# Two units' attention joined one unit earlier, with unit 19's transposing transfer ahead of two loads

## The chip, the cores and the metric

One core of a Trainium2 chip runs one launch of the kernel. The metric is the device time of that launch in microseconds; lower is better. A profiled execution gives, for each engine, when each instruction ran: TensorE (matrix products), VectorE, ScalarE, GpSimd, and SyncE, whose queue SP issues transfers.

## What is computed

Linear attention with a decay for each head, in blocks of 64 positions, followed by two matrix products with a leaky Relu between them. Batch 4, 8 heads, 768 positions, head size 64; then 3072 tokens, model width 512, hidden width 2048.

```python
for b in range(nb):
    sl = slice(b * block, (b + 1) * block)
    qb, kb, vb = (q[:, :, sl].copy(), k[:, :, sl].copy(), v[:, :, sl].copy())
    intra = np.einsum('bhic,bhjc->bhij', qb, kb) * Dmask[None]
    intra = np.einsum('bhij,bhjd->bhid', intra, vb)
    inter = np.einsum('bhid,bhde->bhie', qb * lam_pow[None], kv_state)
    out[:, :, sl] = intra + inter
    kb_dec = kb * rev_pow[None]
    kv_state = lam_block[None, :, None, None] * kv_state + np.einsum('bhsd,bhse->bhde', kb_dec, vb)
...
h = x @ w_in
g = np.maximum(h, 0.0) + alpha * np.minimum(h, 0.0)
return (g @ w_out).astype(np.float32)
```

## The kernel before

**Units and chunks.** The attention works on blocks of 128 positions, two of them (256 positions) at a time. A unit is one batch entry, one half of the heads (4 heads) and one such stretch of 256 positions; there are 24 units, numbered 0 to 23. Four units make a chunk `c` of 512 tokens: chunk 3 is units 12 to 15, chunk 4 is 16 to 19, chunk 5 is 20 to 23. The raw inputs are loaded for a pair of units, `load(c, bi, x)`; `(4, 0)` serves units 16 and 17, `(4, 1)` 18 and 19, `(5, 0)` 20 and 21, `(5, 1)` 22 and 23.

**The second part.** For chunk `c`, `up(c, f)` (L527) makes 128 of the 2048 hidden values for the chunk's 512 tokens: four matmuls into a PSUM bank, a Relu on ScalarE (L540), and on VectorE the operation that makes the leaky Relu `g` (L549). The bank is free when VectorE has read it. `down(c, t, part, 4)` (L556) makes a quarter of the output sums of 128 tokens: four matmuls with four of the sixteen `g`. Parts 0 to 3 of one `t` accumulate in the bank "op"; after part 3 ScalarE copies the sums to `o_sb` and SP stores them. Part `p` reads the `g` numbered 4p to 4p+3. A chunk's `up` needs the attention output `xT` of its four units; `down` of a chunk runs while the next chunk's `up` does.

**What a unit needs.** `prepared(n)` casts k, q and v to 16 bits (k and v on GpSimd, q on ScalarE) and makes the decayed keys on GpSimd. `turned(n)` transposes q and k with one DMA transfer on SP's queue into a tile `qkT` (three buffers, so unit n takes the one of unit n-3). `decayed(n)` multiplies the transposed q with the decay on GpSimd. `states` and `states2` carry the running states on VectorE.

**Stages of attention.** `cluster(old, new)` (L474) puts on TensorE the output of one unit and the scores and state products of another: inter-block products of `old` (L371), scores of `new` (L387), products of masked scores with v of `old` (L412), state products of `new` (L432). VectorE then masks the scores (L398), ScalarE copies the output to `xT`. `cluster2(olds, news)` (L676) does it for up to two old and two new units; the second new unit's scores go into the two "h" banks (L644) and are masked in two halves (L658). Before, `cluster(15, 16)` is the last stage with one new unit, and the joined stages are 16/17+18, 17+18/19+20, 19+20/21, 21/22+23 and 22+23/none.

**Banks.** PSUM has two banks "h" that rotate, one "op", one "tk", two for scores "s", and `acc` (two banks). The second accumulator of joined stages (`acc2`) takes "tk" from `second()` (L597) on.

**Order.** The program's order is written by hand and every engine runs its own instructions in that order; the tile framework inserts the waits. From chunk 3 on, a string of U and D gives the order of `up(c, ...)` and `down(c-1, ...)`, and a table gives what is issued ahead of a position ("step") in it: loads and `turned` on SP, casts on GpSimd and ScalarE, stages on TensorE. GpSimd, ScalarE, VectorE and SP each run in order, so a wait holds what is behind it on that engine.

Of the kernel before, what the change touches and what calls it, by code (L numbers as in the profile page):

```python
# [11 lines left out]
def kernel(  # L12
# [67 lines left out]
    def load(c, bi, x, half=None, queue="S"):  # L80

        pb, b = c // 2, 2 * (c % 2) + bi
        if (c, bi) not in raws:
            raws[c, bi] = [raw_pool.tile([128, H, 2 * D], fp32, tag=f"{n}raw", name=f"{n}raw") for n in "kqv"]
        heads = ds(0, H) if half is None else ds(4 * half, 4)
        i = "kqv".index(x)
        (nc.gpsimd if queue == "G" else nc.sync).dma_start(
            out=raws[c, bi][i][:, heads, :],
            in_=(k, q, v)[i][b, heads, ds(pb * W, W), :].rearrange("h (p e) d -> p h (e d)", e=2),
        )  # L90
# [191 lines left out]
    def engine(x):  # L282
        return nc.gpsimd if x == "G" else nc.vector
# [62 lines left out]
    def decayed(n, eng="G"):  # L346
        c, bi, hh = units[n]
        t = T[n]
        qdT = qkt_pool.tile([128, 2, 2, L], fp16, tag="qdT", name="qdT")
        p = ds(64, 64) if c < 2 else ds(0, L)  # L350
        engine(eng).tensor_tensor(  # L351
            out=qdT[:, :, :, p],
            in0=(t["qps"] if eng == "P" else t["qkT"][:, 0])[:, :, :, p],
            in1=qdecay[:, hh, :, :, p],
            op=ALU.mult,
        )
        t["qdT"] = qdT
# [6 lines left out]
    def inter(n):  # L364
        co, bo, ho = units[n]
        pbo, bb = co // 2, 2 * (co % 2) + bo
        for a in range(2):
            if 2 * pbo + a == 0:
                continue
            for hp in range(2):  # L370
                nc.tensor.matmul(  # L371
                    ot[a][:, hp, :].rearrange("p (e j) -> p e j", e=2),
                    lhsT=R[bb, ho, 2 * pbo + a][:, hp].rearrange("p l d -> p (l d)"),
                    rhs=T[n]["qdT"][:, :, hp, ds(a * 64, 64)],
                    start=(hp == 0),
                    stop=False,
                    skip_group_check=True,
                )

    def score_products(n):  # L380
        t = T[n]
        t["s"] = ps.tile([128, 2, 2, 2, L], fp32, tag="s", name="s")
        for hp in range(2):
            for e in range(2):
                for a, hl in QUADS:
                    p = ds(hl * 64, 64)
                    nc.tensor.matmul(  # L387
                        t["s"][ds(a * 64, 64), hl, hp, 1 - e, :].rearrange("p (e j) -> p e j", e=2),
                        lhsT=t["qkT"][p, 1, e, hp, ds(a * 64, 64)],
                        rhs=t["qkT"][p, 0, :, hp, ds(a * 64, 64)],  # L390
                        start=True,
                        stop=True,
                    )

    def masked(n):
        t = T[n]
        t["sm"] = sm_pool.tile([128, 2, 2, 2, L], fp16, tag="sm", name="sm")
        nc.vector.tensor_tensor(  # L398
            out=t["sm"].rearrange("p a h x j -> p (a h) x j"),
            in0=t["s"].rearrange("p a h x j -> p (a h) x j"),  # L400
            in1=mask_of(units[n][2]),
            op=ALU.mult,
        )

    def intra(n):
        t = T[n]
        pb = units[n][0] // 2
        for hp in range(2):
            for e in range(2):
                for hl, a in QUADS:  # L410
                    p = ds(a * 64, 64)
                    nc.tensor.matmul(  # L412
                        ot[a][ds(hl * 64, 64), hp, :],
                        lhsT=t["v16"][p, 2 * hp + hl, e, :],
                        rhs=t["sm"][p, hl, hp, 1 - e, :],
                        start=(2 * pb + a == 0 and hp == 0 and e == 0),
                        stop=(e == 1),
                        skip_group_check=True,
                    )
# [54 lines left out]
    def cluster(old, new, eng="A"):  # L474

        if old is not None:
            inter(old)
        if new is not None:
            score_products(new)
        if old is not None:  # L480
            intra(old)
        if new is not None:
            state_products(new, kv_acc, old is None)
            masked(new)
        if old is not None:
            attended(old, eng)
        if new is not None:
            states(new, kv_acc)
# [38 lines left out]
    def up(c, f, bi=None, bank="h"):  # L527
        h_ps = bank_of(bank, "h_ps")
        n = CH if bi is None else W
        for gi in range(NHP):  # L530
            x = XT[c][:, gi]
            nc.tensor.matmul(  # L532
                h_ps[:, 0:n] if bi is None else h_ps[:, 0:n].rearrange("p (e j) -> p e j", e=2),
                lhsT=w_in_sb[:, gi, ts(f, 128)],
                rhs=x.rearrange("p e b j -> p (e b j)") if bi is None else x[:, :, bi, :],
                start=(gi == 0),
                stop=(gi == NHP - 1),
            )
        m = m_pool.tile([128, CH], fp32, tag="m", name="m")
        nc.scalar.activation(m[:, 0:n], h_ps[:, 0:n], AF.Relu, scale=-1.0)  # L540
        if (c, f) not in G:
            G[c, f] = g_pool.tile([128, 2, 2, L], fp16, tag=f"g{f}", name=f"g{f}")
        g = G[c, f]
        if bi is None:
            g, mv, hv = g.rearrange("p e b j -> p (e b j)"), m, h_ps
        else:
            g = g[:, :, bi, :]
            mv, hv = (y[:, 0:n].rearrange("p (e j) -> p e j", e=2) for y in (m, h_ps))
        nc.vector.scalar_tensor_tensor(  # L549
            out=g, in0=mv, scalar=oma[:, f : f + 1], in1=hv, op0=ALU.mult, op1=ALU.add  # L550
        )
# [124 lines left out]
    def cluster2(olds, news):  # L676

        for i, n in enumerate(olds):
            inter_in(n, out_of(i), i == 1)
        if news:  # L680
            score_products(news[0])
        for i, n in enumerate(olds):
            intra_in(n, out_of(i))
        for i, n in enumerate(news):
            state_products(n, kv_of(i), i == len(olds))
        if len(news) == 2:
            s = [bank_of("h", "s2").rearrange("p (h x j) -> p h x j", h=2, x=2) for _ in range(2)]
            scores_in(news[1], s)
        if news:
            masked(news[0])  # L690
        if len(news) == 2:
            masked_in(news[1], s)
        for i, n in reversed(list(enumerate(olds))):
            attended_in(n, out_of(i), "A" if i == 0 else "AA")

    def states2(news):
        for i, n in enumerate(news):
            states(n, kv_of(i))
# [295 lines left out]
    up(2, 6, None, "h")  # L994
    up(2, 9, None, "op")
    decayed(16, "G")
    cluster(15, 16, "A")
    cast(17, "v16", "G")
    up(2, 7, None, "tk")
    transposes(17, "D", False)  # L1000
    cast(18, "q16", "A")
    cast(18, "v16", "G")
# [2 lines left out]
    def prepared(n):  # L1005
        casts(n, "GAG")

    def turned(n):
        transposes(n, "D", False)

    plan = {
        3: (
            "UDUDUDUD" + "DDUUDUDUDUDUDUD" + "DDUUDUUDU",
            {
                0: lambda: (turned(18), load(5, 0, "k"), load(5, 0, "q"), prepared(19)),
                2: lambda: (load(5, 0, "v"), decayed(17)),
                5: lambda: turned(19),
                8: lambda: (cluster2([16], [17, 18]), load(5, 1, "k")),
                10: lambda: (prepared(20), load(5, 1, "q")),
                12: lambda: (states2([17, 18]), decayed(18)),  # L1020
                14: lambda: (turned(20), load(5, 1, "v")),
                15: lambda: prepared(21),
                19: lambda: turned(21),
                23: lambda: cluster2([17, 18], [19, 20]),
                25: lambda: decayed(19),
                27: lambda: (states2([19, 20]), decayed(20)),
                28: lambda: prepared(22),
                32: lambda: (cluster2([19, 20], [21]), turned(22)),
            },
        ),  # L1030
        4: (
            "DDUUDUDUDUDUDUD" + "DDUUDUDUDUDUDUD" + "UU",
            {
                2: lambda: (states2([21]), prepared(23)),
                5: lambda: decayed(21),
                7: lambda: turned(23),
                15: lambda: cluster2([21], [22, 23]),
                17: lambda: decayed(22),
                19: lambda: states2([22, 23]),
                20: lambda: decayed(23),  # L1040
# [51 lines left out]
```

## Time and profile before

| | us |
|---|---|
| median of 3 runs | 210.68 |
| lowest and highest | 210.61, 210.79 |
| profiled execution | 210.83 |
| its span, first to last instruction | 209.1 |
| VectorE, ScalarE, GpSimd busy | 132.4, 110.8, 84.3 |

The span is what the trace shows; the rest of the execution's time lies around it. Times inside the trace are counted from the span's start. In the order of time of an engine a row gives start, length, engine, line of the kernel, operation, output and inputs, tile shape, and how many instructions are merged; in brackets stands how long the engine was idle before and what ended it. A group of matmuls ends later than the next begins, since they are pipelined: the distance of two starts is what a group costs. "SPq" is SP issuing a transfer; the time to landing counts from the issue's start.

### The profile page before, as it was taken

The page shows a single profiled execution, that of the slowest core. Times are in us where ns is not written, and L with a number is a line of the kernel's source. Part 1 is how long each engine was busy: PE and PEld are TensorE (multiplying, and loading weights), DVE is VectorE, ACT ScalarE, POOL GpSimd, SP SyncE. Part 2 cuts the span into 40 slices and gives each one's busy share as a digit, 9 for nine tenths or more (in the row PEclk, how much of TensorE's full clock was granted, in tenths as well). Part 3 has the DMA queues.
Part 4 walks back from the last instruction along what each step waited for, and adds up shares of the span by engine and source line. Part 5 has one row for each costly group of instructions (what it writes and reads, how often), then busy time and mean ns, then how long its engine had stood idle before and what let it go on. Part 6 is the DMA issues. An engine that isn't in the chain of part 4 may idle for free.

```text
span 209.1 us, 5240 instructions
## 1 busy us (share of the span) xinstructions
PE 204.0 (98%) x2151; PEld 109.3 (52%) x2151; DVE 132.4 (63%) x233; ACT 110.8 (53%) x207; POOL 84.3 (40%) x114
## 2 busy tenths in 40 slices
PE   7999999999999999999999999999999999999993
PEld 6776455456445465555554464544544444444453
DVE  7978889488789466999956656744674344444000
ACT  7986778154876127666844544643454544344121
POOL 8999793052476983381902938022000000000000
PEclk9999999999999999999999999999999999999999
DMA  6999999998999998999199990404110100111113
GB/s 159 277 197 239 245 253 206 241 282 260 269 211 262 196 241 184 252 209 221 28 220 229 298 211 1 103 0 103 50 48 5 50 39 11 53 52 50 51 50 103
DMA packets 56716, 32.20 MB, mean 154 GB/s; under 512 B 22948, under 2 KB 53044, under 8 KB 56692
## 3 DMA queue, kind: packets, MB, share of 16 engines
q1 hardware_dynamic: 45764, 23.34, 46.4%
q0 software_dynamic: 10912, 8.52, 23.4%
q8 instruction: 17, 0.28, 0.6%
q14 instruction: 7, 0.06, 0.1%
q10 hardware_dynamic: 16, 0.00, 0.0%
HBM read 27.27 MB, written 6.29 MB: 161 GB/s over the span
## 4 chain that ended last, share of the span: by engine, by line
PE 92%; DVE 3%; ACT 2%; issue 1%; ACTq 0%
PE h_ps L532 39%; PE o_ps L562 33%; PE o_ps L585 7%; PE s L387 3%; PE acc L412 2%; PE tpx L337 2%; PE acc L371 2%; DVE dmask L200 1%; PE acc L432 1%; PE acc L629 1%; PE acc L615 1%; ACT qk L248 1%; ACT L178 1%; ACT xT L248 1%; DVE kdec L289 1%
## 5 line engine op out<-in xcount | busy, mean ns | idle before, releaser
L549 DVE SCALAR_TENSOR_TENSOR g<-m,oma,h_ps 128x512 f16<-128x512 f32 (+1 forms) x98 | 71.2, 736 | 46.3 <-ACT m L540 43.3
L532 PE MATMUL h_ps<-xT,w_in_sb 128*128 128x512 f16 (+1 forms) x392 | 91.4, 375 | 0.1
L540 ACT ACTIVATE m<-h_ps 128x512 f32<-128x512 f32 (+1 forms) x98 | 57.3, 588 | 51.0 <-PE h_ps L532 50.5
L562 PE MATMUL o_ps<-w_out_sb,g 128*128 128x512 f16 x320 | 79.0, 379 | 0.0
L532 PEld LDWEIGHTS <-w_in_sb 128*128 128x128 f16 x392 | 37.9, 98 | 43.6 <-issue 0.5
L562 PEld LDWEIGHTS <-g 128*128 128x128 f16 x320 | 29.9, 98 | 34.1 <-DVE g L549 0.2
L398 DVE TENSOR_TENSOR sm<-s,dmask 128x1024 f16<-128x1024 f32 x21 | 25.6, 1221 | 12.4 <-PE s L387 11.7
L351 POOL TENSOR_TENSOR qdT<-qkT,qdecay 128x512 f16<-128x512 f16 (+1 forms) x19 | 20.5, 1083 | 17.3 <-PE h_ps L532 7.2
L248 ACT ACTIVATE xT<-acc 128x512 f16<-128x512 f32 (+1 forms) x27 | 14.2, 550 | 22.6 <-PE acc L432 19.4
L575 ACT ACTIVATE o_sb<-o_ps 128x512 f32<-128x512 f32 (+2 forms) x26 | 14.7, 564 | 15.9 <-PE o_ps L585 10.9
L289 POOL TENSOR_TENSOR kdec<-kraw,kdecay 128x512 f16<-128x512 f32 x18 | 19.7, 1102 | 6.0 <-DMA kraw<-in_k_dram 6.0
L461 DVE SCALAR_TENSOR_TENSOR R<-R,rdecay,acc 128x128 f16<-128x128 f16 x54 | 15.3, 342 | 0.0
L252 POOL CAST qk<-qraw 128x512 f16<-128x512 f32 x12 | 7.4, 614 | 17.1 <-DMA qraw<-in_q_dram 16.2
L252 POOL CAST qk<-kraw 128x512 f16<-128x512 f32 x14 | 8.6, 614 | 13.9 <-DMA kraw<-in_k_dram 10.1
L585 PE MATMUL o_ps<-w_out_sb,g 128*128 128x512 f16 (+2 forms) x96 | 14.1, 308 | 0.0
L585 PEld LDWEIGHTS <-g 128*128 128x128 f16 x96 | 8.1, 98 | 6.1
L387 PE MATMUL s<-qkT 64*64 64x128 f16 x336 | 8.8, 221 | 0.1
L276 POOL DMA_DIRECT2D v<-in_v_dram x11 | 8.6, 792 | 0.0
L248 ACT ACTIVATE qk<-qraw 128x512 f16<-128x512 f32 x11 | 6.9, 624 | 2.7 <-DMA qraw<-in_q_dram 2.1
L252 POOL CAST v<-vraw 128x512 f16<-128x512 f32 x10 | 6.1, 615 | 5.4 <-DMA vraw<-in_v_dram 5.4
L387 PEld LDWEIGHTS <-qkT 64*64 64x64 f16 x336 | 5.8, 106 | 2.1 <-issue 0.4
L248 ACT ACTIVATE qkT<-tpx 128x512 f16<-128x512 f16 x11 | 6.5, 598 | 0.8 <-PE tpx L337 0.8
(76 smaller groups left out, 133.5 us busy)
## 6 DMA issues: line engine op xcount, KB each, us to landing
out_dram<-o_sb SPq DMA_DIRECT2D x23, 256.0 KB, 2.3
kraw<-in_k_dram SPq DMA_DIRECT2D x7, 512.0 KB, 5.6
qraw<-in_q_dram SPq DMA_DIRECT2D x6, 512.0 KB, 5.9
w_in_sb<-in_moe_w_in_dram POOLq DMA_DIRECT2D x4, 512.0 KB, 8.0
w_out_sb<-in_moe_w_out_dram POOLq DMA_DIRECT2D x4, 512.0 KB, 10.6
vraw<-in_v_dram SPq DMA_DIRECT2D x7, 256.0 KB, 5.7
qraw<-in_q_dram POOLq DMA_DIRECT2D x6, 256.0 KB, 7.2
qraw<-in_q_dram SPq DMA_DIRECT2D x6, 256.0 KB, 4.8
```

What stands on the lines that cost most here:

```text
L248: nc.scalar.activation(out, in_, AF.Copy)
L252: nc.gpsimd.tensor_copy(out=out, in_=in_)
L289: engine(eng).tensor_tensor(out=kdec, in0=kr, in1=kdecay[:, ds(4 * hh, 4), :].rearrange("p h e -> p e h").unsqueeze(3).to_broadcast([128, ...
L351: engine(eng).tensor_tensor(out=qdT[:, :, :, p], in0=(t["qps"] if eng == "P" else t["qkT"][:, 0])[:, :, :, p], in1=qdecay[:, hh, :, :, p], ...
L387: nc.tensor.matmul(t["s"][ds(a * 64, 64), hl, hp, 1 - e, :].rearrange("p (e j) -> p e j", e=2), lhsT=t["qkT"][p, 1, e, hp, ds(a * 64, 64)] ...
L398: nc.vector.tensor_tensor(out=t["sm"].rearrange("p a h x j -> p (a h) x j"), in0=t["s"].rearrange("p a h x j -> p (a h) x j"), in1=mask_of ...
L461: nc.vector.scalar_tensor_tensor(out=R[b, hh, m + 1][:, hp], in0=R[b, hh, m][:, hp], scalar=rdecay[:, 2 * hh + hp : 2 * hh + hp + 1], in1= ...
L532: nc.tensor.matmul(h_ps[:, 0:n] if bi is None else h_ps[:, 0:n].rearrange("p (e j) -> p e j", e=2), lhsT=w_in_sb[:, gi, ts(f, 128)], rhs=x ...
L540: nc.scalar.activation(m[:, 0:n], h_ps[:, 0:n], AF.Relu, scale=-1.0)
L549: nc.vector.scalar_tensor_tensor(out=g, in0=mv, scalar=oma[:, f : f + 1], in1=hv, op0=ALU.mult, op1=ALU.add)
L562: nc.tensor.matmul(o_ps, lhsT=lhs(c, f, t), rhs=w_out_sb[:, f, :], start=(f == 0), stop=(f == NF - 1),)
L585: nc.tensor.matmul(o_ps[:, 0:n], lhsT=lhs(c, f, t), rhs=w_out_sb[:, f, ds(x, n)], start=(f == 0), stop=(f == NF - 1),)
```

## The change

`cluster(15, 16)` is left out of the list ahead of the plan, and `cluster2([15], [16, 17])` stands at step 3 of chunk 3's part; the joined stages then are 15/16+17, 16+17/18+19, 18+19/20+21, 20+21/22+23 and 22+23/none. The order string of chunk 3 begins with three D, and `up(2, 7)` goes to a bank "h" in place of "tk". `turned(19)` is issued right after that first joined stage, and the loads of k and q of `(5, 0)` behind it, where they stood ahead of it at step 0; the load of v goes from step 2 to 6. Loads, casts, transfers and decays of units 18 to 23 move by some steps.

```diff
     up(2, 9, None, "op")
     decayed(16, "G")
-    cluster(15, 16, "A")
     cast(17, "v16", "G")
-    up(2, 7, None, "tk")
+    up(2, 7, None, "h")
     transposes(17, "D", False)
...
         3: (
-            "UDUDUDUD" + "DDUUDUDUDUDUDUD" + "DDUUDUUDU",
+            "DDD" + "DUUDUDUDUUD" + "DDUUDUDUDUUDUUDUUD",
             {
-                0: lambda: (turned(18), load(5, 0, "k"), load(5, 0, "q"), prepared(19)),
-                2: lambda: (load(5, 0, "v"), decayed(17)),
-                5: lambda: turned(19),
-                8: lambda: (cluster2([16], [17, 18]), load(5, 1, "k")),
-                10: lambda: (prepared(20), load(5, 1, "q")),
-                12: lambda: (states2([17, 18]), decayed(18)),
-                14: lambda: (turned(20), load(5, 1, "v")),
-                15: lambda: prepared(21),
-                19: lambda: turned(21),
-                23: lambda: cluster2([17, 18], [19, 20]),
-                25: lambda: decayed(19),
-                27: lambda: (states2([19, 20]), decayed(20)),
-                28: lambda: prepared(22),
-                32: lambda: (cluster2([19, 20], [21]), turned(22)),
+                0: lambda: (turned(18), prepared(19)),
+                2: lambda: decayed(17),
+                3: lambda: (cluster2([15], [16, 17]), turned(19), load(5, 0, "k"), load(5, 0, "q")),
+                6: lambda: load(5, 0, "v"),
+                7: lambda: states2([16, 17]),
+                9: lambda: prepared(20),
+                14: lambda: (cluster2([16, 17], [18, 19]), load(5, 1, "k")),
+                16: lambda: (turned(20), load(5, 1, "q"), decayed(18)),
+                18: lambda: (states2([18, 19]), prepared(21)),
+                20: lambda: (load(5, 1, "v"), decayed(19)),
+                22: lambda: turned(21),
+                27: lambda: prepared(22),
+                32: lambda: (cluster2([18, 19], [20, 21]), turned(22)),
             },
         ),
         4: (
             "DDUUDUDUDUDUDUD" + "DDUUDUDUDUDUDUD" + "UU",
             {
-                2: lambda: (states2([21]), prepared(23)),
-                5: lambda: decayed(21),
-                7: lambda: turned(23),
-                15: lambda: cluster2([21], [22, 23]),
+                3: lambda: prepared(23),
+                4: lambda: states2([20, 21]),
+                5: lambda: decayed(20),
+                6: lambda: decayed(21),
+                8: lambda: turned(23),
+                15: lambda: cluster2([20, 21], [22, 23]),
                 17: lambda: decayed(22),
```

## The prediction

> **What bounds the kernel now.** I read the first page, then the table of stretches, then the order of time of each engine around the change. From the page: the span, TensorE's share of it, and the chain of waits by engine.
>
> ```profile
> span 209.1 us, 5240 instructions
> PE 204.0 (98%) x2151; PEld 109.3 (52%) x2151; DVE 132.4 (63%) x233; ACT 110.8 (53%) x207; POOL 84.3 (40%) x114
> PE 92%; DVE 3%; ACT 2%; issue 1%; ACTq 0%
> ```
>
> TensorE is busy for 204.0 of 209.1 us and holds 92% of the chain. The table says where the rest is not. Its columns are the stretch, its length, then each engine's busy time, the granted clock, the DMA share and the rate.
>
> ```profile
> core 0: us, PE busy (x) PEld busy (x) DVE busy (x) ACT busy (x) POOL busy (x), PEclk, DMA share, GB/s
> 99.69:115.29 15.60, 15.54 (x174) 7.91 (x173) 11.46 (x19) 8.48 (x15) 6.73 (x10) 1.00 0.77 166
> 115.29:191.87 76.58, 76.58 (x590) 37.14 (x589) 39.93 (x62) 36.44 (x65) 13.84 (x16) 1.00 0.26 69
> ```
>
> From 115.29 to 191.87 us TensorE never pauses, at clock 1.00. So nothing behind 115 can give time back: each us by which TensorE is held up at 100 to 115 comes out at the end, and each us of its work that is saved there does too. The question is only what the change does to TensorE's work and to its waits. TensorE's order of time around the place, with start and length:
>
> ```profile
> 96.23 3.63 PE L532 MATMUL h_ps<-xT,w_in_sb 128*128 128x512 f16 x16
> 99.69 0.39 PE L371 MATMUL acc<-qdT,R 128*128 128x128 f16 x4
> ...
> 104.17 1.03 PE L562 MATMUL o_ps<-w_out_sb,g 128*128 128x512 f16 x4
> 105.25 1.02 PE L532 MATMUL h_ps<-xT,w_in_sb 128*128 128x512 f16 x4
> ...
> 114.42 1.02 PE L532 MATMUL h_ps<-xT,w_in_sb 128*128 128x512 f16 x4
> ```
>
> Four groups of four matmuls take 99.69 - 96.23 = 3.46, so one "U" or "D" takes 0.865 us. The D at 104.17 was done at 105.03; the U behind it starts at 105.25, a wait of 0.22.
>
> **TensorE's own work.** No matmul is added or taken away; the products are grouped into four joined stages and the last one, where there were five and the last one. The five, from the first inter-block product to the next large matmul:
>
> ```profile
> 99.69:100.70 1.01, 1.01 (x45) 1.00 0.57 128
> 108.70:110.06 1.36, 1.36 (x69) 1.00 1.15 304
> 123.06:124.87 1.81, 1.81 (x90) 1.00 0.41 97
> 132.65:134.10 1.45, 1.45 (x65) 1.00 0.46 153
> 147.06:148.43 1.37, 1.37 (x70) 1.00 0.00 0
> sum 7.00, PE 7.00; mean PE 1.40
> ```
>
> In order they are units 15/16 (one output, one score), 16/17+18, 17+18/19+20, 19+20/21, 21/22+23. After the change they are 15/16+17, then 16+17/18+19, 18+19/20+21 and 20+21/22+23: one of 1.36 and three of 1.81, together 6.79. Saved: **0.21 us**. Bounds: 0.20 to 0.22, since the two stages of one output and two scores differ by 0.01.
>
> **First wait: the bank of the output sums.** up(2,9) writes the single bank "op"; the next writer is the first D. Between them stood a stage of 1.01, up(2,7) and the first U. Now only up(2,7) is left. Without a wait the first D would start at 99.69 + 0.865 = 100.55. VectorE's rows:
>
> ```profile
> 100.85 0.74 DVE L549 SCALAR_TENSOR_TENSOR g<-m,oma,h_ps 128x512 f16<-128x512 f32 x1
> 104.45 0.75 DVE L549 SCALAR_TENSOR_TENSOR g<-m,oma,h_ps 128x512 f16<-128x512 f32 x1 [0.15 <-ACT m L540]
> 109.49 1.23 DVE L398 TENSOR_TENSOR sm<-s,dmask 128x1024 f16<-128x1024 f32 x1
> 110.63 0.68 DVE L658 TENSOR_TENSOR sm<-s,dmask 128x512 f16<-128x512 f32 x1
> ```
>
> The first row is up(2,9)'s last reader, done at 101.59; it is late because the mask and states of unit 15 sit before four such rows, and none of that changes. The second row gives the hand-over: it ends at 105.20 and the waiting U starts at 105.25. So the first D starts at 101.64: a wait of **1.09 us**. Behind it on TensorE stand two more D, the joined stage and all that follows. Bounds: 1.04 without the hand-over, 1.14 with twice it. The next thing late would be up(2,7)'s output, wanted by the last matmul of the second D at 103.1. Its Relu cannot start before 100.55 and the vector operation after it ends near 102.3, so it costs nothing.
>
> The 0.22 at 105.25 goes away. It came from three casts (units 18 and 19) that ScalarE ran ahead of the first U's Relu; now three D cover them, 2.6 us against 1.6 of casts. Without that cover it would be back: 0.22.
>
> **Second wait: one D where there were two.** The joined stage starts at 101.64 + 2.59 = 104.23. In the row of the same shape VectorE starts the mask 0.79 after the stage does (109.49 against 108.70) and ends the first half of the second mask at 111.31, 2.61 after. That half frees the first "h" bank. Behind the stage stood two D (1.36 + 1.73 = 3.09, later than 2.66); now one D stands there and ends at 2.23. The U starts 2.66 after the stage, at 106.89: a wait of **0.43**. The second half is off in time, 0.60 later against 0.865. Unit 15's attention output, copied by ScalarE in between, ends before that. The other three stages have two D behind them. The row of that shape:
>
> ```profile
> 124.29 1.23 DVE L398 TENSOR_TENSOR sm<-s,dmask 128x1024 f16<-128x1024 f32 x1 [0.52 <-PE acc L629]
> ```
>
> The mask starts 1.23 into a stage of 1.81 that began at 123.06, since its output tile is still read; the half mask is done 1.82 later, at 3.05, and the U is due at 1.81 + 1.73 = 3.54: nothing there.
>
> **Third wait: the q load behind ScalarE's cast.** This is the term with the wide bounds. The queue SP in order of time, then the landing times of the first transposing transfer and of the q load, and the rate at which two loads later moved:
>
> ```profile
> 103.47 1.24 SPq L307 DMA_TRANSPOSE qkT<-qk  x1
> 104.76 0.58 SPq L87 DMA_DIRECT2D kraw<-in_k_dram  x1
> 105.39 0.63 SPq L87 DMA_DIRECT2D qraw<-in_q_dram  x1
> 106.07 1.68 SPq L87 DMA_DIRECT2D vraw<-in_v_dram  x1
> 107.90 4.35 SPq L307 DMA_TRANSPOSE qkT<-qk  x1
> ```
>
> ```profile
> qkT<-qk SPq DMA_TRANSPOSE x1, 3.2
> qraw<-in_q_dram SPq DMA_DIRECT2D x1, 512.0 KB, 7.0
> DMA packets 2144, 1.08 MB, mean 307 GB/s; under 512 B 88, under 2 KB 2136, under 8 KB 2144
> ```
>
> Before, unit 18's transposing transfer went at 103.47, k and q of (5,0) right behind, and q landed at 105.39 + 7.0 = 112.4. Now unit 19's goes between. It writes the buffer that held unit 16's q and k, so it waits until unit 16's scores are done, 0.79 into the stage: 105.02. Behind it on SP stand k, q, a store and v. What waits for q is unit 20's cast on ScalarE; behind that stand the Relus, which VectorE and then TensorE wait for.
>
> ```profile
> 112.48 0.63 ACT L248 ACTIVATE qk<-qraw 128x512 f16<-128x512 f32 x1 [2.06 <-DMA qraw<-in_q_dram]
> 113.01 0.58 ACT L540 ACTIVATE m<-h_ps 128x512 f32<-128x512 f32 x1
> 113.62 0.75 DVE L549 SCALAR_TENSOR_TENSOR g<-m,oma,h_ps 128x512 f16<-128x512 f32 x1 [1.72 <-ACT m L540]
> ```
>
> Here ScalarE already waited 2.06 us, harmless: it fell beside the stage and two D. From landing (112.4) over cast, Relu and vector operation to the U at 114.42 is 2.0 us. Now the cast stands at step 9, in the midst of U's. From 106.89 the steps run U U D U D U D U U, so step 12's U is due at 106.89 + 8 × 0.865 = 113.81, and it takes the bank of step 9's U, whose Relu is behind the cast. From the issue of a transposing transfer to the landing of the q that follows is 112.4 - 103.47 = 8.9: q lands at 105.02 + 8.9 = 113.9, the U can start at 115.9, a wait of **2.1**. Least: the transfer lands 3.2 after 105.02 and the two loads (1.05 MB) run at 307 GB/s, 3.4 more: 111.6, and no wait. Most: the store of 256 KB shares the engines and adds 0.26/0.307 = 0.85, a wait of 3.0. I take 2.1, since v is again queued behind q as in the row, and the same three loads follow one transposing transfer.
>
> The rest is covered. Two groups of the page's list give GpSimd's pace:
>
> ```profile
> L351 POOL TENSOR_TENSOR qdT<-qkT,qdecay 128x512 f16<-128x512 f16 (+1 forms) x19 | 20.5, 1083 | 17.3 <-PE h_ps L532 7.2
> L289 POOL TENSOR_TENSOR kdec<-kraw,kdecay 128x512 f16<-128x512 f32 x18 | 19.7, 1102 | 6.0 <-DMA kraw<-in_k_dram 6.0
> ```
>
> Its cast of unit 20's v waits for the load behind q; with 3.4 us for that load, more than its share, and 1.1 for each of three operations, it is through near 121, and the stage that reads the results is at step 32, past 130. Units 20 to 23 have their loads, casts and transfers asked for at least five steps (4.3 us) ahead, with transfers of 3.2. The stages that ask for two units more need no new bank: at steps 14 and 32 both "h" banks are free a step and the stage's first 1.2 us earlier. If that cover failed, a wait like the second, 0.4, would follow.
>
> **Sum.** -0.21 - 0.22 + 1.09 + 0.43 + 2.1 = +3.2 us. The profiled execution took 210.83 (span 209.1 and 1.7 around it), 0.15 above the median of 210.68; against it the sum is 214.0, against the median **213.9**. With the bounds, +1.1 to +4.1.
>
> **The rivals.** (1) The q load is in time: the third wait is nothing, +1.1, **211.8**. It decides by q landing before 111.8. For it: the two loads alone need 3.4 us. Against: q took 7.0 in its row, most of it with the engines full. A rule of the Trainium skill, Advanced Engine Details and Errata, section X-Bar Transpose, points to this case: transposing transfers are as fast as plain ones, 350 to 400 GB/s expected, by which I estimate 0.7 us for 256 KB and a q in time. The trace does not agree so far: 3.2 us to landing. (2) The transposing transfer holds SP long: unit 19's took 4.35 where it stood behind three loads, not 1.24. Then k and q go 3.1 later, the third wait is 5.2 and the time **217.0**. Against: ahead of the loads only unit 18's is before it, and that one went in 1.24. (3) Not slower: the waits are absorbed. Place: TensorE between 115 and 192. If it had slack of 3.6 us there, set by another engine's pace, the three waits would vanish into it and -0.43 be left, **210.3**; from less than 3.2 of slack on, slower. For it: only that matmul ends are modelled. Against: 76.58 of 76.58 busy.
>
> **Chances.** The forecast 0.74 (its own range 212.7 to 214.9), rival 1 0.14, rival 2 0.06, rival 3 0.06. From the forecast's upper bound down to rival 1: 211.7 to 214.9, which leaves out rivals 2 and 3 and a little of the forecast. Within 0.2% (0.42 us, about what repeated runs can tell): 0.02, from rival 3 with part of the waits; faster: 0.04; slower: 0.94.
>
> **What would show it.** In the changed kernel: the first D starts about 1.1 after up(2,7) ends and right behind up(2,9)'s vector operation; the first U of that part stands 0.4 behind its D, right behind a half mask; SP issues two transposing transfers in a row, the second as unit 16's scores end; ScalarE waits near 2.8 us for q, and step 12's U some 2 us for VectorE; the joined stages take 1.4 and three times 1.8. Wrong: a first D without a gap, a cast of q without a wait, or a TensorE gap behind step 14.

## The result, and the profile after

| | us |
|---|---|
| before, median of 4 | 210.74 |
| after, median of 4 (lowest, highest) | 213.44 (212.57, 214.06) |
| ratio, 95% interval | 1.0123 [1.0102, 1.0145] |
| profiled execution after | 212.57 (span 210.8) |

The kernel became 2.7 us slower. The profiled execution is the fastest of the four, and that matters below. From the page of the changed kernel:

```profile
span 210.8 us, 5238 instructions
PE 204.0 (97%) x2151; PEld 109.6 (52%) x2151; DVE 132.4 (63%) x234; ACT 110.7 (53%) x208; POOL 84.3 (40%) x114
...
PE 86%; DVE 6%; DMA 3%; ACT 2%; SPq 1%; issue 1%; ACTq 0%
```

TensorE is busy for the same 204.0 us with the same 2151 matmuls, in a longer span: what came was waiting. The chain that ended last now runs through VectorE for 6% (3% before), through a transfer for 3% and through SP's queue for 1%, which it did not before. Its order of time in the changed kernel (start, length, instructions, idle time and what ended it):

```profile
95.72 4.49 PE L532 MATMUL h_ps<-xT,w_in_sb 128*128 128x512 f16 x20
101.14 2.75 PE L562 MATMUL o_ps<-w_out_sb,g 128*128 128x512 f16 x12 [0.92 <-DVE g L549]
103.73 0.39 PE L615 MATMUL acc<-qdT,R 128*128 128x128 f16 x4
...
105.09 1.04 PE L562 MATMUL o_ps<-w_out_sb,g 128*128 128x512 f16 x4
106.39 1.89 PE L532 MATMUL h_ps<-xT,w_in_sb 128*128 128x512 f16 x8 [0.26 <-DVE sm L658]
...
112.43 1.03 PE L532 MATMUL h_ps<-xT,w_in_sb 128*128 128x512 f16 x4
114.46 1.02 PE L532 MATMUL h_ps<-xT,w_in_sb 128*128 128x512 f16 x4 [1.01 <-DVE g L549]
```

All three waits are there, each ended by the instruction of VectorE that was named. For the first two these are VectorE's rows:

```profile
99.69 1.40 DVE L549 SCALAR_TENSOR_TENSOR g<-m,oma,h_ps 128x512 f16<-128x512 f32 x2
105.65 0.68 DVE L658 TENSOR_TENSOR sm<-s,dmask 128x512 f16<-128x512 f32 x1
```

The second instruction of the first row is up(2,9)'s; it ends at 101.09 and the first D starts at 101.14. The half mask ends at 106.33 and the waiting U starts at 106.39. The brackets count from the modelled end of the last matmul, which is about 0.17 after the next group could start; counted from that start they are 101.14 - (95.72 + 5 × 0.865) = 1.10, 106.39 - (105.09 + 0.865) = 0.43, and 114.46 - (112.43 + 0.865) = 1.17. The queue SP and ScalarE's cast of unit 20's q:

```profile
104.60 1.23 SPq L307 DMA_TRANSPOSE qkT<-qk  x1
105.88 1.11 SPq L87 DMA_DIRECT2D kraw<-in_k_dram  x1
107.04 0.58 SPq L87 DMA_DIRECT2D qraw<-in_q_dram  x1
107.73 1.15 SPq L578 DMA_DIRECT2D out_dram<-o_sb  x1
108.92 0.43 SPq L87 DMA_DIRECT2D vraw<-in_v_dram  x1
```

```profile
112.52 0.63 ACT L248 ACTIVATE qk<-qraw 128x512 f16<-128x512 f32 x1 [1.88 <-DMA qraw<-in_q_dram]
113.05 1.07 ACT L540 ACTIVATE m<-h_ps 128x512 f32<-128x512 f32 x2
```

Unit 19's transfer goes at 104.60, 0.87 after the stage began (0.79 was forecast); ScalarE waits 1.88 us for q, and two Relus stand behind the cast.

One stretch serves to compare executions, since what lies ahead of it and behind it is the same program: from the start of the stage of units 14 and 15 to that of the last joined stage. It contains all that the change touches. The columns are the stretch, its length, TensorE's busy time, the granted clock, the DMA share and the rate. Before, then after:

```profile
95.21:161.39 66.18, 66.12 (x654) 1.00 0.52 116
```

```profile
94.71:163.13 68.42, 66.23 (x653) 1.00 0.52 112
```

It is 2.24 us longer, and the terms add up to that: -0.21 - 0.25 + 1.10 + 0.43 + 1.17 = 2.24. The 0.25 are the wait of 0.22 that the prediction took away and one of 0.03 at 114.42 before, ahead of the same cast, that it did not count. The profiled executions' whole times differ by only 212.57 - 210.83 = 1.74, because this one reached the stretch 0.50 earlier (94.71 against 95.21), in code that is alike.

### The profile page after: what moved, and what is told of

It reads as the page before. It is cut to its first block, busy times and chain, and to the rows that moved or that the text cites. A ratio compares the mean times of both kernels' runs of the same rounds, so it can differ in the third digit from the quotient of the medians.

```text
span 210.8 us, 5238 instructions
## 1 busy us (share of the span) xinstructions
PE 204.0 (97%) x2151; PEld 109.6 (52%) x2151; DVE 132.4 (63%) x234; ACT 110.7 (53%) x208; POOL 84.3 (40%) x114
## 4 chain that ended last, share of the span: by engine, by line
PE 86%; DVE 6%; DMA 3%; ACT 2%; SPq 1%; issue 1%; ACTq 0%
PE h_ps L532 35%; PE o_ps L562 32%; PE o_ps L585 7%; PE s L387 3%; DMA qraw<-in_q_dram 3%; DVE g L549 2%; PE acc L412 2%; PE tpx L337 2%; PE acc L371 1%; DVE dmask L200 1%; PE acc L615 1%; PE acc L629 1%; PE acc L432 1%; SPq L307 1%; ACT L178 1%
## 5 line engine op out<-in xcount | busy, mean ns | idle before, releaser
L398 DVE TENSOR_TENSOR sm<-s,dmask 128x1024 f16<-128x1024 f32 x20 | 24.4, 1221 | 15.4 <-PE s L387 13.8
L387 PE MATMUL s<-qkT 64*64 64x128 f16 x320 | 8.3, 221 | 0.1
```

The costliest lines, as they stand in the source:

```text
L387: nc.tensor.matmul(t["s"][ds(a * 64, 64), hl, hp, 1 - e, :].rearrange("p (e j) -> p e j", e=2), lhsT=t["qkT"][p, 1, e, hp, ds(a * 64, 64)] ...
L398: nc.vector.tensor_tensor(out=t["sm"].rearrange("p a h x j -> p (a h) x j"), in0=t["s"].rearrange("p a h x j -> p (a h) x j"), in1=mask_of ...
```

## The experiments

The table has each run's median, its ratio with the 95% interval, the stretch of its profiled execution, and the three waits there, worked out as above. Each ratio is taken against the executions of the kernel before that ran with it, so it is not the quotient of the medians shown. The first row is the kernel before, the second the changed one; stretch and waits are of one execution each.

| | median | ratio | stretch | first | second | third |
|---|---|---|---|---|---|---|
| before | 210.74 | | 66.18 | | | 0.03 |
| after | 213.44 | 1.0123 [1.0102, 1.0145] | 68.42 | 1.10 | 0.43 | 1.17 |
| after again | 213.55 | 1.0134 [1.0108, 1.0160] | 68.78 | 1.10 | 0.43 | 1.53 |
| two banks swapped | 212.60 | 1.0094 [1.0068, 1.0120] | 68.32 | 0 (0.25 at the second D) | 0.43 | 1.92 |
| stage at step 2 | 212.09 | 1.0070 [1.0047, 1.0093] | 67.50 | 1.10 | 0 | 0.67 |
| loads first | 212.01 | 1.0062 [1.0040, 1.0085] | 67.25 | 1.09 | 0.43 | 0 |
| cast at step 13 | 211.75 | 1.0056 [1.0037, 1.0075] | 67.25 | 1.10 | 0.43 | 0 |
| four buffers | 212.42 | 1.0077 [1.0057, 1.0096] | 67.78 | 1.10 | 0.43 | 0.53 |
| v right behind q | 213.43 | 1.0120 [1.0085, 1.0156] | 68.81 | 1.10 | 0.43 | 1.56 |
| before, transfer first | 211.51 | 1.0024 [1.0009, 1.0039] | 66.95 | | | 0.81 |
| all three taken away | 210.39 | 0.9976 [0.9962, 0.9990] | 65.75 | 0 | 0 | 0 |

### The first wait: two banks swapped

```diff
-    up(2, 3, None, "tk")
+    up(2, 3, None, "op")
     up(2, 6, None, "h")
-    up(2, 9, None, "op")
+    up(2, 9, None, "tk")
```

> The changed kernel with two banks swapped: up(2,3) writes "op", up(2,9) writes "tk". Theory of three waits: the first D no longer waits for up(2,9)'s vector operation; a small wait of some 0.2 us may show at the second D, for up(2,7)'s output. Unit 16's scores, unit 19's transposing transfer and the q load all come 0.9 us earlier with it, so the third wait keeps its size: about 212.5 us, 0.9 below the changed kernel. Rival (q's landing does not hang on the stage): step 12's U waits 0.9 longer in its place, and the time stays near 213.4.

Measured: 212.60. In its order of time the first D starts where the five ups end (96.43 + 4.32):

```profile
96.43 4.49 PE L532 MATMUL h_ps<-xT,w_in_sb 128*128 128x512 f16 x20
100.75 3.00 PE L562 MATMUL o_ps<-w_out_sb,g 128*128 128x512 f16 x12
```

Three D take 2.59; the next stage starts 2.84 after 100.75, so the small wait of 0.25 at the second D is there too. The bank was the cause of the first wait. Whether the gain is passed on to the end, this run alone does not show. Its median is 0.84 below the changed kernel's, but the two intervals overlap ([1.0068, 1.0120] and [1.0102, 1.0145]), and the profiled execution, the slowest of its four (213.40), has a third wait of 1.92, where the same size as before was expected. Unit 19's transfer did go earlier with the stage, 0.88 after its start (104.47 against 103.59); but ScalarE's cast of q came 8.7 after the transfer's issue (113.12 - 104.47), where it was 7.9 in the changed kernel.

### The second wait: the stage a step earlier

```diff
-                2: lambda: decayed(17),
-                3: lambda: (cluster2([15], [16, 17]), turned(19), load(5, 0, "k"), load(5, 0, "q")),
+                2: lambda: (decayed(17), cluster2([15], [16, 17]), turned(19), load(5, 0, "k"), load(5, 0, "q")),
```

> The changed kernel with the first joined stage, turned(19) and the two loads at step 2 in place of 3, so that two D stand behind the stage and two ahead of it. Theory: the second wait (0.43 us) goes; unit 16's scores, and with them unit 19's transfer and q, come 0.86 earlier while step 12's U comes 0.43 earlier, so the third wait shrinks by 0.4 too: 0.8 to 0.9 below the changed kernel, about 212.6 us. Rival (the wait behind the stage is not the mask's): it stays, and the time with it, near 213.4.

Measured: 212.09, more gain than expected. Behind the stage stand two D, and the U's follow without a gap:

```profile
104.55 1.90 PE L562 MATMUL o_ps<-w_out_sb,g 128*128 128x512 f16 x8
106.28 1.89 PE L532 MATMUL h_ps<-xT,w_in_sb 128*128 128x512 f16 x8
...
113.86 1.02 PE L532 MATMUL h_ps<-xT,w_in_sb 128*128 128x512 f16 x4 [0.50 <-DVE g L549]
```

The second wait is gone, and the third is 0.67, 0.50 to 0.86 less than in the two profiles of the changed kernel, where 0.43 was worked out.

### The third wait: the cast out of the way, the loads first, the gate open

```diff
-                9: lambda: prepared(20),
+                13: lambda: prepared(20),
```

> The changed kernel with prepared(20) at step 13 in place of 9, so that ScalarE's cast of unit 20's q stands behind the Relu of step 12's U. Theory: q lands as late as before, but no Relu is behind the cast; no wait at step 12: 211.4 to 212.2 us, and the executions lie closer together than the changed kernel's 212.6 to 214.1, since what varies is q's landing. Rival (the wait comes from something else than the cast): near 213.4 with the same spread.

```diff
-                3: lambda: (cluster2([15], [16, 17]), turned(19), load(5, 0, "k"), load(5, 0, "q")),
+                3: lambda: (cluster2([15], [16, 17]), load(5, 0, "k"), load(5, 0, "q"), turned(19)),
```

> The changed kernel with the loads of k and q of (5,0) ahead of turned(19) again, all else as changed. Theory: the loads follow unit 18's transfer at about 103.3 us, q lands near 111, ScalarE does not wait for it and step 12's U starts at once; the first two waits stay: 211.4 to 212.2 us. Rival 1 (the order of the queue does not set the third wait): near 213.4. Rival 2 (the transposing transfer behind the loads comes too late for the stage at step 14): a new wait there, up to 2 us, and again near 213.4.

Measured: 211.75 with the late cast and 212.01 with the loads first. In both the U's of steps 11 and 12 follow each other without a gap, as one row of eight matmuls. With the late cast:

```profile
112.63 1.89 PE L532 MATMUL h_ps<-xT,w_in_sb 128*128 128x512 f16 x8
```

With the loads first ScalarE's cast starts without a wait:

```profile
111.17 0.63 ACT L248 ACTIVATE qk<-qraw 128x512 f16<-128x512 f32 x1
```

Both stretches are 67.25, what the first two waits leave: 66.18 - 0.46 + 1.10 + 0.43 = 67.25. So the third wait hangs on the cast's place, and q's lateness on the place of unit 19's transfer in the queue. Behind the loads that transfer made no new wait at step 14. The executions with the late cast lie within 0.74 us (211.57 to 212.31), but those of the kernel before lie within 1.34 (210.12 to 211.46, 23 of them), so the spread says nothing.

```diff
-    kv_pool = ctx.enter_context(tc.tile_pool(name="kvh", bufs=8))
-    qkt_pool = ctx.enter_context(tc.tile_pool(name="qkt", bufs=3))
+    kv_pool = ctx.enter_context(tc.tile_pool(name="kvh", bufs=7))
+    qkt_pool = ctx.enter_context(tc.tile_pool(name="qkt", bufs=4))
+    qdt_pool = ctx.enter_context(tc.tile_pool(name="qdt", bufs=3))
...
-        qdT = qkt_pool.tile([128, 2, 2, L], fp16, tag="qdT", name="qdT")
+        qdT = qdt_pool.tile([128, 2, 2, L], fp16, tag="qdT", name="qdT")
```

> The changed kernel with four buffers for qkT (qdT keeps three, in a pool of its own; v and decayed keys have seven buffers instead of eight to make room). Unit 19's transposing transfer then need not wait for unit 16's scores and goes right behind unit 18's, near 103.2 us. Theory (the gate by the scores makes q late): q lands near 112, the third wait falls to 0.0 to 0.5: about 212 us. Rival (the transfer's own time makes q late, not its start): the third wait stays 1.2 or more: near 213.4.

Measured: 212.42, third wait 0.53. Unit 19's transfer now goes at 103.74, right behind unit 18's, though the stage begins only at 104.15:

```profile
103.74 1.24 SPq L308 DMA_TRANSPOSE qkT<-qk  x1
105.03 0.59 SPq L88 DMA_DIRECT2D kraw<-in_k_dram  x1
...
114.24 1.02 PE L533 MATMUL h_ps<-xT,w_in_sb 128*128 128x512 f16 x4 [0.37 <-DVE g L550]
```

So, by these single profiles, the gate by unit 16's scores makes 0.6 to 1.0 of the third wait, and the other 0.53 is left by the transfer's place ahead of the loads; with the loads first it is gone as well.

### One part of the change in the kernel before

```diff
-                0: lambda: (turned(18), load(5, 0, "k"), load(5, 0, "q"), prepared(19)),
+                0: lambda: (turned(18), prepared(19), turned(19), load(5, 0, "k"), load(5, 0, "q")),
                 2: lambda: (load(5, 0, "v"), decayed(17)),
-                5: lambda: turned(19),
```

> The kernel before with one part of the change alone: turned(19) at step 0 ahead of the loads of k and q of (5,0), not at step 5. Its buffer is free there, so it goes right behind unit 18's transfer. Theory (the transfer itself holds the loads back, as 3 us do): q lands 0.5 to 1.5 us later than before, near 113 to 114, where the Relu behind the cast was due at 112.9: 211.0 to 211.9 us. Rival (a transposing transfer is as fast as a plain one, and only the gate by unit 16's scores makes the changed kernel's q late): no more than 0.2 us over before, 210.7 to 210.9.

Measured: 211.51, ratio 1.0024 [1.0009, 1.0039] over ten executions. Its transfer of unit 19 is issued right behind unit 18's, ScalarE then waits longer for q, and a U waits 0.81 for VectorE where it had waited 0.03:

```profile
qkT<-qk SPq DMA_TRANSPOSE x1, 4.7
```

```profile
112.78 0.63 ACT L248 ACTIVATE qk<-qraw 128x512 f16<-128x512 f32 x1 [2.84 <-DMA qraw<-in_q_dram]
```

```profile
114.73 1.02 PE L532 MATMUL h_ps<-xT,w_in_sb 128*128 128x512 f16 x4 [0.65 <-DVE g L549]
```

So the transfer's place ahead of the loads makes q late without any gate: 0.8 us at the place where it shows. The rival's 0.2 us falls by the profile; the interval's lower end, 0.19 us, does not exclude it by itself. But this run does not set a transposing transfer apart from a plain one: at the 307 GB/s of the prediction's row, 256 KB would hold the engines for 0.85 us by estimate, about as long, and a plain transfer in that place was not tried. What the trace of the kernel before does show is a lower rate while the engines were busy: first packets of unit 18's transfer alone (104.8 to 105.3 us), then packets that are nearly all of loads (107.95 to 112):

```profile
DMA packets 419, 0.11 MB, mean 215 GB/s; under 512 B 419, under 2 KB 419, under 8 KB 419
DMA packets 2467, 1.21 MB, mean 300 GB/s; under 512 B 154, under 2 KB 2467, under 8 KB 2467
```

The transposing packets are smaller; whether the rate is low for that or for the transposing was not tried, and a last part of unit 19's transfer moved at 287 GB/s in the changed kernel (107.45 to 107.75). The transfer also held the loads back by pausing: in this run the engines moved 10 GB/s between 107.0 and 108.1, though k's load was issued at 105.70. The packets of the loads begin at 108.2; in the kernel before they begin at 106.0.

### The size of the third wait

> The changed kernel unaltered, for the same chip as the three below and for a second profile. Theory: the first two waits are the same in every execution (1.07 and 0.43 us, set by instructions), the third differs with q's landing, 1.0 to 2.6, and carries the spread of 212.6 to 214.1: median 213 to 213.7. Rival: the spread comes from ahead of the change, and the third wait is the same 1.2 us again.

Measured: 213.55. Its profiled execution has the same first and second wait and 1.53 for the third, and it reached the stretch at 95.14, not 94.71: both theories are partly right. Two profiles differ by 0.36 in the third wait and by 0.43 in what lies ahead of the change.

In these two profiles the cast starts 7.9 and 8.3 us after unit 19's transfer is issued (112.52 - 104.60, 113.30 - 105.03), and 8.7 in the one with two banks swapped; the kernel before had 9.0 for unit 18's (112.48 - 103.47). Was it v, queued right behind q before?

```diff
-                3: lambda: (cluster2([15], [16, 17]), turned(19), load(5, 0, "k"), load(5, 0, "q")),
+                3: lambda: (cluster2([15], [16, 17]), turned(19), load(5, 0, "k"), load(5, 0, "q"), load(5, 0, "v")),
-                6: lambda: load(5, 0, "v"),
```

> The changed kernel with the load of v of (5,0) at step 3 right behind q's, as in the kernel before, not at step 6 behind a store. In two profiles of the changed kernel q landed 7.9 and 8.2 us after unit 19's transfer was issued, not the 8.9 that the kernel before showed for unit 18's. Theory (there v was queued right behind q and shared the engines with it; a store and v come later here): with v right behind, q lands near 8.9 again, the third wait is near 2.1 and the time 213.9 to 214.5 us. Rival (v's place does nothing to q): the third wait stays 1.1 to 1.6 and the time near 213.5.

Measured: 213.43, third wait 1.56. Unit 19's transfer was issued at 105.23, and:

```profile
113.53 0.63 ACT L248 ACTIVATE qk<-qraw 128x512 f16<-128x512 f32 x1 [2.27 <-DMA qraw<-in_q_dram]
```

That is 8.3 again. My theory fell: v's place does nothing that shows. Why q took 9.0 behind unit 18's transfer and 7.9 to 8.7 behind unit 19's stays open; the 9.0 is from one execution, and the others differ by 0.8 among themselves.

### All three taken away

```diff
-    up(2, 3, None, "tk")
+    up(2, 3, None, "op")
     up(2, 6, None, "h")
-    up(2, 9, None, "op")
+    up(2, 7, None, "tk")
...
-    up(2, 7, None, "h")
+    up(2, 9, None, "h")
...
-                2: lambda: decayed(17),
-                3: lambda: (cluster2([15], [16, 17]), turned(19), load(5, 0, "k"), load(5, 0, "q")),
+                2: lambda: (decayed(17), cluster2([15], [16, 17]), turned(19), load(5, 0, "k"), load(5, 0, "q")),
...
-                9: lambda: prepared(20),
+                13: lambda: prepared(20),
```

> The changed kernel with all three waits taken away: up(2,3) in "op", up(2,7) ahead of up(2,9) in "tk" with up(2,9) last in "h", the first joined stage at step 2, prepared(20) at step 13. Theory: what is left is the saving of the joined stages (0.21 us) and of the wait of 0.22 in the kernel before: 210.3 us, ratio 0.998. Rival (joined stages move waits to later steps that the three now hide): 211 us or more.

Measured: 210.39 (209.86 to 210.61, 12 executions), ratio 0.9976 [0.9962, 0.9990]: faster than both kernels. The stretch has no idle time at all:

```profile
95.16:160.91 65.75, 65.75 (x654) 1.00 0.52 116
```

Against 66.18 that is 0.43 less, and 0.21 + 0.22 were expected. No wait moved to a later step. Unit 19's transfer still goes ahead of the loads here; the late cast covers it.

## Why the prediction was right

- **What bounds it.** Right: every stretch of the changed kernel and its variants in the table is 65.75, TensorE's own work, plus the waits listed, within 0.04. The rival that slack behind 115 us absorbs the waits fell.
- **TensorE's work.** The joined stages take 1.36 (103.73 to 105.09) and 1.81 in the changed kernel, and the stretch without waits is 0.43 shorter than before: -0.21 and the old waits of 0.25 make -0.46, of which 0.43 were forecast.
- **First wait.** 1.09 forecast, 1.10 measured; removed by swapping banks, and the 0.25 that this brings at the second D was worked out from the same rows.
- **Second wait.** 0.43 and 0.43; removed by a second D behind the stage.
- **Third wait.** The mechanism was right (the gate, the queue, the cast, the Relus behind it), the size was off: 2.1 forecast, 1.17 and 1.53 measured, within the bounds of 0 and 3.0. The term is the time from the issue of the transposing transfer to the landing of q, taken as 8.9 from the one row there was; counted to the start of the cast it was 9.0 there, and 7.9 and 8.3 in the changed kernel's two profiles, 0.7 to 1.1 shorter. With 1.35, the mean of the two third waits, the sum would have been 213.1, not 213.9. Measured was 213.44; the 0.3 between lies within the 1.5 that the four executions span.
- **Rivals.** A kernel without the third wait (211.8) is what the late cast and the loads first made, 211.75 and 212.01. The transfer that holds SP for 4.35 did not come: 1.23; with the loads ahead of it, it did hold SP, for 3.12. As to the rule of the Trainium skill, Advanced Engine Details and Errata, section X-Bar Transpose, that transposing transfers are as fast as plain ones: the trace does not agree, with 215 GB/s for unit 18's packets against 300 for the loads while the engines were busy, and q was not in time: ScalarE waited 1.88 us for it.

## What to carry to other kernels

Where one engine is busy without a gap, regrouping its work saves only what its own rows say (here 0.21 us), while bringing a bank's next writer close to its last reader costs a wait for the other engines to read the bank (here 1.10 and 0.43 us). So check three distances before moving a stage: from a bank's writer to the next writer of that bank, from the stage to the next user of the banks it borrows, and from a load's issue to the in-order instruction that waits for it. An operation that waits for a load belongs behind the work that others wait for, not ahead of it; moving one cast by four steps took away a wait of 1.2 to 1.5 us.

## What the runs showed of the hardware

Two transposing transfers issued one behind the other did not take the same time: unit 18's landed 3.1 us after its issue in both profiles of the changed kernel, unit 19's after 3.9 in the first of them. There, unit 18's and then unit 19's:

```profile
qkT<-qk SPq DMA_TRANSPOSE x1, 3.1
```

```profile
qkT<-qk SPq DMA_TRANSPOSE x1, 3.9
```

In that profile unit 19's packets paused: the engines moved 10 GB/s from 106.6 to 107.4, though k's load was issued at 105.88, and the loads moved only behind the last of them, from 107.8. All eight profiles in which a packet of 16 KB of the instruction queue (0.9 to 1.3 us long, at 105.65 in this one) started before the last packets of unit 19's transfer have such a pause, of 0.8 to 1.5 us. With four buffers that packet started at 106.74, behind them, and there was none. Whether it is the cause was not tried. Nor is the second transfer always the slower one: in the version with all three waits taken away they took 4.7 and then 4.2. And executions differ in code without any change: the stage of units 14 and 15 began between 94.71 and 95.41 us in the eleven profiles, 0.70 apart, more than the 0.43 that the last version gains, which only the stretch and many executions could show.
